# Sorting the columns of K and P by head inside VectorE's transposes (decode attention plus MLP, one core)

## The chip, the cores and the metric

The kernel runs on one core of a Trainium2 chip. The metric is the device time of one execution in microseconds (us); a kernel's time is the median of several executions. A core has TensorE (PE: matmuls, with PEld for the loading of their weights), VectorE (DVE), ScalarE (ACT), GpSimd (POOL) and SyncE (SP, which here issues most of the DMAs and waits for them). Each works through its own instructions in order and waits for the others at semaphores.

## The reference

One token (x has 1024 values) goes through an attention branch and an MLP branch, and both are added to x. The sizes are fixed: 32 query heads, 4 heads of K and V (8 query heads share one), 128 values per head, and the last 4096 positions of the cache.

```python
D, Hq, Hkv, Sk, Dh, F = 1024, 32, 4, 65536, 128, 3584
W = min(4096, max(256, Sk // 4))            # 4096
xn = layernorm(x)
q = (xn @ wq).reshape(1, 1, Hq, Dh).transpose(0, 2, 1, 3)
k = repeat(k_cache[:, :, Sk - W:, :], 8, axis=1)
v = repeat(v_cache[:, :, Sk - W:, :], 8, axis=1)
p = softmax(einsum("bhqd,bhkd->bhqk", q, k) * Dh ** -0.5)
a = einsum("bhqk,bhkd->bhqd", p, v).transpose(0, 2, 1, 3).reshape(1, 1, Hq * Dh) @ wo
y = layernorm(xn)
b = gelu(y @ w1 + b1) @ w2 + b2
out = x + a + b
```

## The kernel before, in words

Everything that is loaded is used once: w1, w2 (7 MB each), wq, wo (8 MB each), and 4 MB each of K and V, some 40 MB in all. The order of the loads is written out by hand on SP's queue. W1, K and wq are issued at the start; w2 (into w1's place) and V when the rows of w1 are done; wo (into wq's place, in pieces of 20, 8, 3 and 1 rows) when the rows of q are done.

**How K lies.** The window of 4096 keys is cut into 32 stretches (m) of 128 keys (b). Partition m*4+g holds stretch m of head g: 128 keys of 128 values. So every group of 32 partitions holds eight stretches of all four heads. VectorE's transpose works on blocks of 32 by 32; for TensorE the 128 values of a key (four pieces, e, of 32) must lie along the partitions. `turn_k` (L320, the transpose itself at L325) does it in eight instructions (n) of 16 keys each, 2048 columns: a block of 32 partitions (m, g) by 32 values becomes 32 partitions (values) by 32 columns (m, g). The columns of KD are then in the order n, e, b, m, g, so that the four heads alternate from column to column. KD and the loaded K (KR) share the space KV, shifted by one instruction's 2048 columns, so that each transpose writes over what the one before it has read.

**Scores.** `scores(g)` (L468) does for one head eight matmuls (L472, through the helper line L333) of 512 columns each, into bank g of PSUM. The view KG (L466) picks head g: every fourth column of KD. The stationary side is LB, a block pattern of q that lines L445 and L446 write. Ahead of that the rows of q are copied out of PSUM (L419 on ACT, L421 on DVE), turned on TensorE (L425), copied to QT (L429) and spread (L435).

**Softmax.** The maximum over the columns (L488), its transpose on TensorE (L478), the maximum over the pieces (L494, L499), its spread (L483) and the bias (L505) go in two halves of two heads each. Then ACT takes the exponentials, one instruction of 512 columns for each head (L510), and writes them as bf16 into Pb: column x*4+g for head g, so every fourth column. The sums go into SUMS on the way.

**P times V.** Two transposes on VectorE (L540, 1024 columns each) turn Pb's blocks of 32 by 32 into PT, and eight instructions (L546 on DVE, L547 on ACT) gather and mask them into PG, the stationary side of the product with V. The loop over V (`pv_rows`) follows. Its result goes through L579, L582 and L589, and L595 writes it as OT, two columns for each value of the heads, into VEC. L575 is a matmul into a bank that is not read. Last is the loop over wo (seven trips of four rows, and four rows behind it), which waits for the pieces of wo through SP (L600).

**The order around the change.** On VectorE: the GELU of the MLP (to L408), the eight K transposes, L421, L429, L445, the maxima, the P transposes, half of the gathering, L582, L595. On TensorE: the rows of w1, the rows of q, the q transposes, the scores with the maxima's small matmuls between them, the loop over w2, the loop over V, the loop over wo. On ACT: L419, L446, L499 and L505, the exponentials of the first half, L499 of the second half, L505, the exponentials of the second half, half of the gathering.

Of the kernel before, what the change touches and what calls it, by code (L numbers as in the profile page):

```python
# [7 lines left out]
ACTF = mybir.ActivationFunctionType  # L8
# [5 lines left out]
HKV = 4  # L14
# [14 lines left out]
NB = W // MB // 2  # L29
# [22 lines left out]
def bass_parallel_sum__sliding_block_cached__mixer_channel_mlp__decode_kernel(  # L52
# [18 lines left out]
    pe, dve, act, pool, sp = nc.tensor, nc.vector, nc.scalar, nc.gpsimd, nc.sync  # L71
# [12 lines left out]
    DVE = Track(nc, "S_DVE")  # L84
# [49 lines left out]
    KD = KV[:, 0:HKV * W]  # L134
    KR = KV[:, 2048:2048 + HKV * W]
    V = KV[:, 2048 + HKV * W:2048 + 2 * HKV * W]
    Pb = KV[:, HKV * W:HKV * W + 2048]
    PT = KV[:, 0:2048]
# [6 lines left out]
    PS = nc.alloc_psum_tensor("PS", [128, 8 * 512], f32)  # L145
# [11 lines left out]
    C = {}  # L157
# [94 lines left out]
    def fold(out, at, n):  # L252
# [9 lines left out]
        out=SAME[:, :].rearrange("p (h q) -> p h q", q=4), in0=HD[:, 112:120].unsqueeze(2).to_broadcast([128, REP, 4]),  # L262
# [52 lines left out]
    C["y"] = DVE.mark(dve.tensor_scalar(out=YTb[:, 0:KC], in0=YT16[:, 0:8], scalar1=msy[:, 2:3], scalar2=msy[:, 7:8],  # L315
                                        op0=ALU.subtract, op1=ALU.mult))
    C["zq"] = C["zo"] = DVE.mark(dve.memset(PS[:, 4 * 512:8 * 512], 0.0))
    KD4 = KD.rearrange("p (n e b s) -> p n b e s", n=8, e=4, b=16)

    def turn_k(n):  # L320
        if n == 0:
            dve.wait_ge(s_k, 16)
        else:
            dve.wait_ge(DVE.sem, DVE.cnt)
        C["kd"] = DVE.mark(dve.transpose(  # L325
            out=KD4[:, n], in_=KR[:, n * 2048:(n + 1) * 2048].rearrange("p (b e s) -> p b e s", b=16, e=4)))


    def lowered(ap, weights):
# [12 lines left out]
    def full(out, lhsT, rhs, load, start=False):  # L342
        return tile(out, lhsT, rhs, (128, 128), (0, 0), load, start)
# [42 lines left out]
    for i in range(8):  # L386
        n = 128 if i < 4 else 96
# [4 lines left out]
    for b, c in ((0, 4), (1, 3)):  # L392
# [16 lines left out]
        out=GT, in0=HT[:, :].unsqueeze(2).to_broadcast([128, FC, 2]), in1=U2[:, :].unsqueeze(2).to_broadcast([128, FC, 2]),  # L409
        op=ALU.mult))  # L410

    for n in range(8):
        turn_k(n)
# [49 lines left out]

    pe.wait_ge(DVE.sem, C["lb", 1])
    pe.wait_ge(ACT.sem, C["lb", 3])
    KG = KD.rearrange("p (n e x g) -> p e g n x", n=8, e=4, g=HKV)  # L466

    def scores(g):  # L468
        for c in range(2):
            for e in range(4):  # L470
                at = (e * HKV + g) * WIN + 8 - 8 * c
                last = full(PS[:, g * 512:(g + 1) * 512], LB[:, at:at + 128],  # L472
                            KG[:, e, g, 4 * c:4 * c + 4, :], True, c + e == 0)
        C["sc"] = PE.mark(last)
# [28 lines left out]
    def weigh(half):  # L503
        act.wait_ge(PE.sem, C["mxb"])
        C["bias"] = ACT.mark(act.activation(  # L505
            out=BIAS[:, 2 * half:2 * half + 2], in_=PS[:, 6 * 512 + 128 + 2 * half:6 * 512 + 130 + 2 * half],
            func=ACTF.Copy, scale=-SCALE))
        act.wait_ge(ACT.sem, C["bias"])
        for g in range(2 * half, 2 * half + 2):
            C["exp"] = ACT.mark(act.activation(  # L510
                out=Pb.rearrange("p (x g) -> p g x", g=HKV)[:, g, :], in_=PS[:, g * 512:(g + 1) * 512], func=ACTF.Exp,
                bias=BIAS[:, g:g + 1], scale=SCALE, accum_out=SUMS[:, g:g + 1]))

    scores(0)
# [6 lines left out]
    take_max(1)  # L521
    spread_max(0)
    weigh(0)
    sp.wait_ge(PE.sem, C["q"])
    load_rows(WA, wo_p, WO_CHUNKS, D, s_wo)
# [6 lines left out]
    join_max(1)  # L532
    spread_max(1)
    weigh(1)
    PT4 = PT.rearrange("p (b u c h) -> p b u c h", u=2, c=2, h=REP)[:, :, 0]
    PG4 = PG.rearrange("p (b c g h) -> p g b c h", c=2, g=HKV, h=REP)
    HB = NB // 2
    dve.wait_ge(ACT.sem, C["exp"])
    for half in range(2):
        C["tr", half] = DVE.mark(dve.transpose(out=PT[:, half * 1024:(half + 1) * 1024], in_=Pb[:, half * 1024:(half + 1) * 1024]))  # L540
    for half, eng, track in ((0, act, ACT), (1, dve, DVE)):
        eng.wait_ge(DVE.sem, C["tr", half])
        for g in range(HKV):
# [8 lines left out]
        out=SUMX[:, :].rearrange("p (g r) -> p g r", g=HKV), in0=SAME[:, :].unsqueeze(1).to_broadcast([128, HKV, 32]),  # L552
# [28 lines left out]
    for c in range(1, 2):  # L581
        C["d_od"] = DVE.mark(dve.scalar_tensor_tensor(  # L582
            out=OD[:, :], in0=PS[:, 4 * 512 + 128 * c:4 * 512 + 128 * c + 128], scalar=BLK[:, c:c + 1], in1=OD[:, :],
# [4 lines left out]
    for dq in range(4):  # L588
# [7 lines left out]
        out=OT, in0=PS[:, 6 * 512 + 160:6 * 512 + 192].unsqueeze(2).to_broadcast([128, 32, 2]), scalar1=REC[:, 0:1], scalar2=None, op0=ALU.mult))  # L596
# [55 lines left out]
```

## Time and profile before

| | |
|---|---|
| time, median of 3 runs | 103.63 us (103.58 to 103.99) |
| the profiled execution's own time | 102.51 us, span 101.1 us |
| busy, share of the span | PE 49.6 us (49%), DVE 32.4 (32%), PEld 20.5 (20%), ACT 15.1 (15%), POOL 9.1 (9%) |
| read from memory | 39.86 MB, 394 GB/s over the span |
| chain that ended last | DMA 84%, PE 10%, issue 2% |
| eight K transposes (L325) | 18.5 us busy, 2311 ns each |
| 32 score matmuls (L333, KV and LB) | 14.7 us busy, 57.67 to 72.40 us |
| four exponentials (L510) | 5.2 us busy, 1400 ns each |
| two P transposes (L540) | 2.4 us busy, 1224 ns each |

The span runs from the first to the last instruction, and the execution's own time has a little more on both sides. Times in the trace are microseconds from the start of the span. In a line of the profile, `out<-in` names the tensors, then come partitions by elements and type, and how often; the idle time of the engine ahead of it stands with what ended it. KV is the space that K, V and P share, WW the one for the weight matrices, PS is PSUM. The helper line L333 stands for every matmul that `tile`, `put` and `full` issue, so that these are told apart by their tensors.

### The profile page before, as it was taken

Reading aid. Unit: us, or ns where it says so; the run is one execution under the profiler, and the core shown is the slowest. Engines: PE = TensorE matmul, PEld = TensorE weight load, DVE = VectorE, ACT = ScalarE, POOL = GpSimd, SP = SyncE. Lnnn points to the kernel's source line nnn. Section 1 sums busy time; section 2 is a strip of 40 time slices with the busy share of each in tenths; the row PEclk is TensorE's granted clock in tenths of the full one; section 3 lists DMA queues with packets and bytes.
Section 4 is the critical chain, followed back from the end, with each engine's and each line's share of the span. In section 5 each row is a group of like instructions: output and inputs, shape, how many; then the busy total and the mean of one; then the engine's idle time right before and its main releaser. Section 6 shows DMA issues by size and latency. Waiting matters only on the chain.

```text
span 101.1 us, 1321 instructions
## 1 busy us (share of the span) xinstructions
PE 49.6 (49%) x523; PEld 20.5 (20%) x460; DVE 32.4 (32%) x42; ACT 15.1 (15%) x29; POOL 9.1 (9%) x33
## 2 busy tenths in 40 slices
PE   0000031579510000000496499999818857799672
PEld 0000031123110000000121222222215434445441
DVE  0000003360069999999202400221320760011000
ACT  0400000510400000000002200001298470010001
POOL 2000002599400000000000000000000100000000
PEclk9999999999998555555569976999995799999999
DMA  9888899599999999999999889999999699699400
GB/s 340 386 366 363 364 408 659 230 415 415 428 609 415 415 415 415 415 415 415 408 658 386 363 363 408 512 415 428 415 467 502 275 518 502 263 447 384 167 0 1
DMA packets 1340, 39.86 MB, mean 394 GB/s; under 512 B 182, under 2 KB 186, under 8 KB 444
## 3 DMA queue, kind: packets, MB, share of 16 engines
q1 hardware_dynamic: 1300, 39.85, 91.9%
q10 hardware_dynamic: 40, 0.01, 0.0%
HBM read 39.86 MB, written 0.00 MB: 394 GB/s over the span
## 4 chain that ended last, share of the span: by engine, by line
DMA 84%; PE 10%; issue 2%; SPq 1%; ACT 0%
DMA WW<-in_A_wq_dram 47%; DMA WW<-in_A_wo_dram 37%; PE PS L333 10%; SPq L203 1%; SPq L211 0%; ACT ORow L617 0%; SPq L196 0%; SPq L369 0%; SPq L600 0%
## 5 line engine op out<-in xcount | busy, mean ns | idle before, releaser
L325 DVE STREAM_TRANSPOSE KV<-KV 128x2048 bf16<-128x2048 bf16 x8 | 18.5, 2311 | 0.2
L333 PE MATMUL PS<-WW,XNTb 128*32 x64 | 5.2, 481 | 21.3 <-SPq L369 21.3
L333 PE MATMUL PS<-KV,LB 128*128 128x512 bf16 x32 | 14.7, 630 | 1.0 <-DVE LB L445 1.0
L333 PE MATMUL PS<-WW,VEC 128*32 (+1 forms) x240 | 10.2, 309 | 2.5 <-issue 2.3
L288 PE MATMUL PS<-oneb,XBR 1*128 1x1 bf16 x8 | 0.6, 196 | 13.8 <-DMA XBR<-in_A_x_dram 13.8
L333 PEld LDWEIGHTS PS<-WW,VEC 128*32 (+1 forms) x236 | 5.7, 105 | 7.2 <-issue 6.9
L333 PE MATMUL PS<-WW,YTb 128*32 x56 | 5.8, 542 | 1.6 <-DMA WW<-in_B_w_dram 1.6
L333 PE MATMUL PS<-KV 128*64 x64 | 5.0, 278 | 2.3 <-issue 1.2
L333 PEld LDWEIGHTS PS<-WW,XNTb 128*32 x32 | 1.1, 104 | 25.0 <-issue 25.0
L488 DVE TENSOR_REDUCE MXP<-PS 128x2 f32<-128x1024 f32 x2 | 2.4, 1224 | 10.8 <-PE PS L333 10.8
L333 PEld LDWEIGHTS PS<-KV,LB 128*128 128x128 bf16 x32 | 3.6, 116 | 10.8 <-issue 9.7
L510 ACT ACTIVATE KV<-PS,BIAS 128x512 bf16<-128x512 f32 x4 | 5.2, 1400 | 0.1
L551 POOL TENSOR_TENSOR SUMX<-SAME,SUMS 128x128 f32<-128x128 f32 x1 | 0.4, 401 | 52.3 <-ACT KV L510 52.3
L291 DVE COPY XT<-PS 128x8 f32<-128x8 f32 x1 | 0.2, 166 | 14.4 <-PE PS L288 14.4
L419 ACT ACTIVATE Hs<-PS 128x512 bf16<-128x512 f32 x1 | 0.6, 598 | 25.5 <-PE PS L333 25.5
L540 DVE STREAM_TRANSPOSE KV<-KV 128x1024 bf16<-128x1024 bf16 x2 | 2.4, 1224 | 4.6 <-ACT KV L510 4.6
L333 PEld LDWEIGHTS PS<-KV 128*64 x64 | 2.9, 109 | 4.2 <-issue 4.2
L288 PEld LDWEIGHTS PS<-oneb,XBR 1*128 1x128 bf16 x8 | 0.6, 160 | 13.7 <-issue 13.7
L582 DVE SCALAR_TENSOR_TENSOR OD<-PS,BLK,OD 128x128 f32<-128x128 f32 x1 | 0.4, 351 | 7.9 <-ACT OD L579 7.9
L333 PEld LDWEIGHTS PS<-WW,YTb 128*32 x32 | 1.6, 117 | 6.0 <-issue 5.7
L547 ACT ACTIVATE KV<-KV,GM 128x512 bf16<-128x512 bf16 x4 | 2.6, 710 | 1.3 <-DVE KV L540 1.3
L421 DVE CAST Hs<-PS 128x512 bf16<-128x512 f32 x1 | 0.7, 692 | 6.0 <-PE PS L333 6.0
(90 smaller groups left out, 40.0 us busy)
## 6 DMA issues: line engine op xcount, KB each, us to landing
WW<-in_B_w_dram SPq DMA_DIRECT2D x2, 7168.0 KB, 29.5
WW<-in_A_wo_dram SPq DMA_DIRECT2D x1, 5120.0 KB, 33.3
KV<-in_A_k_cache_dram SPq DMA_DIRECT2D x1, 4096.0 KB, 28.7
KV<-in_A_v_cache_dram SPq DMA_DIRECT2D x1, 4096.0 KB, 49.0
WW<-in_A_wo_dram SPq DMA_DIRECT2D x1, 2048.0 KB, 37.8
WW<-in_A_wo_dram SPq DMA_DIRECT2D x1, 768.0 KB, 39.2
WW<-in_A_wo_dram SPq DMA_DIRECT2D x1, 256.0 KB, 39.3
KV<-in_B_b_dram ACTq DMA_DIRECT2D x1, 7.0 KB, 8.8
```

Of the source, the lines that this page charges most:

```text
L203: sp.dma_start(dst[:, :], cache[0, :, SK - W:SK, :].rearrange("g (m b) d -> m g (b d)", m=MB),).then_inc(semaphore, 16)
L288: last = pe.matmul(xt[:, r:r + 1], lhsT=XBR[0:1, r:D:KC], rhs=oneb[0:1, 0:1])
L325: C["kd"] = DVE.mark(dve.transpose(out=KD4[:, n], in_=KR[:, n * 2048:(n + 1) * 2048].rearrange("p (b e s) -> p b e s", b=16, e=4)))
L333: return pe.add_instruction(mybir.InstMatmult(name=nc.get_next_instruction_name(), engine=pe.engine, ins=[lowered(rhs, False), lowered(lhs ...
L419: C["a_qs"] = ACT.mark(act.activation(out=Qs[:, 0:512], in_=PS[:, 6 * 512:7 * 512], func=ACTF.Copy))
L421: C["d_qs"] = DVE.mark(dve.tensor_copy(Qs[:, 512:1024], PS[:, 7 * 512:8 * 512]))
L488: C["mx", half] = DVE.mark(dve.tensor_reduce(out=MXP[:, 2 * half:2 * half + 2], in_=PS[:, half * 1024:(half + 1) * 1024].rearrange("p (g x ...
L510: C["exp"] = ACT.mark(act.activation(out=Pb.rearrange("p (x g) -> p g x", g=HKV)[:, g, :], in_=PS[:, g * 512:(g + 1) * 512], func=ACTF.Exp ...
L540: C["tr", half] = DVE.mark(dve.transpose(out=PT[:, half * 1024:(half + 1) * 1024], in_=Pb[:, half * 1024:(half + 1) * 1024]))
L547: else act.activation(out=dst, in_=src, func=ACTF.Copy, scale=GM[:, g:g + 1]))
L551: C["sumx"] = POOL.mark(pool.tensor_tensor(out=SUMX[:, :].rearrange("p (g r) -> p g r", g=HKV), in0=SAME[:, :].unsqueeze(1).to_broadcast([ ...
L582: C["d_od"] = DVE.mark(dve.scalar_tensor_tensor(out=OD[:, :], in0=PS[:, 4 * 512 + 128 * c:4 * 512 + 128 * c + 128], scalar=BLK[:, c:c + 1] ...
```

## The change

The columns of K and P are sorted by head. In KD the order is now n, e, g, b, m: the 128 columns of one head in one piece lie side by side. The K transpose reads as before and scatters what it writes: of the 32 columns of a block, eight runs over m of the four heads, each element goes 128 columns (256 bytes) from the one before it, and after four heads it goes on with the next m. The score matmuls read runs of 128 columns. The exponentials write 512 columns of Pb side by side for each head. The P transposes read across the four heads (512 columns, 1024 bytes, from one element to the next) and write PT in the order that it had. No instruction is added, removed or moved.

```diff
-    KD4 = KD.rearrange("p (n e b s) -> p n b e s", n=8, e=4, b=16)
+    KD4 = KD.rearrange("p (n e g b m) -> p n b e m g", n=8, e=4, g=HKV, b=16)
...
         C["kd"] = DVE.mark(dve.transpose(
-            out=KD4[:, n], in_=KR[:, n * 2048:(n + 1) * 2048].rearrange("p (b e s) -> p b e s", b=16, e=4)))
+            out=KD4[:, n], in_=KR[:, n * 2048:(n + 1) * 2048].rearrange("p (b e m g) -> p b e m g", b=16, e=4, g=HKV)))
...
-    KG = KD.rearrange("p (n e x g) -> p e g n x", n=8, e=4, g=HKV)
+    KG = KD.rearrange("p (n e g x) -> p e g n x", n=8, e=4, g=HKV)
...
             C["exp"] = ACT.mark(act.activation(
-                out=Pb.rearrange("p (x g) -> p g x", g=HKV)[:, g, :], in_=PS[:, g * 512:(g + 1) * 512], func=ACTF.Exp,
+                out=Pb[:, g * 512:(g + 1) * 512], in_=PS[:, g * 512:(g + 1) * 512], func=ACTF.Exp,
                 bias=BIAS[:, g:g + 1], scale=SCALE, accum_out=SUMS[:, g:g + 1]))
...
     for half in range(2):
-        C["tr", half] = DVE.mark(dve.transpose(out=PT[:, half * 1024:(half + 1) * 1024], in_=Pb[:, half * 1024:(half + 1) * 1024]))
+        C["tr", half] = DVE.mark(dve.transpose(
+            out=PT[:, half * 1024:(half + 1) * 1024].rearrange("p (b m g) -> p b m g", b=HB, g=HKV),
+            in_=Pb.rearrange("p (g b m) -> p b m g", g=HKV, b=NB)[:, half * HB:half * HB + HB]))
```

## The prediction, made before the changed kernel had run

> **What bounds the kernel now.** I read the chain of waits first, then the DMA issues, the timeline around the first wait that the change can reach, the groups by shape, and the granted clock by window. The chain that ended last, in order of time:
>
> ```profile
> 1.91 47.34 DMA WW<-in_A_wq_dram
> ...
> 49.54 5.19 PE PS L333 x62
> ...
> 55.13 37.78 DMA WW<-in_A_wo_dram
> ...
> 93.03 0.62 PE PS L333 x16
> ```
>
> The chip loads memory almost without a break: wq, then 5.2 us of q rows on TensorE, then wo. But the last DMA link is only one of two that end together. Wo comes in four pieces (the DMA issues: size, us from issue to landing; the first and last piece shown, the second takes 37.8):
>
> ```profile
> WW<-in_A_wo_dram SPq DMA_DIRECT2D x1, 5120.0 KB, 33.3
> ...
> WW<-in_A_wo_dram SPq DMA_DIRECT2D x1, 256.0 KB, 39.3
> ```
>
> Issued from 54.75 us on, the first piece (20 of 32 rows, five trips of the wo loop) lands at 88.1, the second at 92.9, the last (issued 56.1) at 95.4. The loop began at 93.03, because attention's last step (OT, L595) ended only at 92.35 and the matmul queued behind it on TensorE (L575, which nothing waits for) at 92.85; the timeline:
>
> ```profile
> 91.95 0.40 DVE L595 TENSOR_SCALAR VEC<-PS,REC 128x64 bf16<-128x64 f32 x1 [1.10 <-PE PS L589]
> ...
> 93.03 0.62 PE L333 MATMUL PS<-WW,VEC 128*32 x16 [0.17 <-SPq L600]
> ```
>
> So a longer attention path lengthens the kernel one for one, while a shorter one soon meets the loads: the last row needs the piece of 95.4, so TensorE could end at about 95.8 instead of 99.33. **The most that can be gained is 3.5 us.** Attention needs the transposed K from VectorE, which has room only here (the timeline of VectorE alone):
>
> ```profile
> 30.03 18.73 DVE L325 STREAM_TRANSPOSE KV<-KV 128x2048 bf16<-128x2048 bf16 x8
> 54.76 0.69 DVE L421 CAST Hs<-PS 128x512 bf16<-128x512 f32 x1 [6.00 <-PE PS L333]
> ```
>
> The eight K transposes are busy until 48.76. Next in VectorE's order is the copy of half of q (L421), which waits for TensorE until 54.76: 6.00 us of slack. Behind it are queued the q transposes, the QT copy, LB and, from 57.67, the score matmuls.
>
> **The change part by part.** No instruction is added or removed; four kinds of access change.
>
> *Score matmuls (L472).* 32 run from 57.67 to 72.40, one every 0.452 us. The windows give a granted clock of 0.50 at 59.5 to 61.5 and 1.00 from 63 on; the pitch is the same in both, so the stride of four elements sets it. Adjacent 512-column reads are the q rows, eight in two rounds of four column groups: a loop step took 0.43 us at full clock (52.43 to 52.86) and 0.80 at half (51.63 to 52.43), 0.215 and 0.40 a round. The q rows began at half clock and were at full after 2.8 us. If the scores do the same: 7 at 0.40 and 25 at 0.215 = 8.2 us against 14.73. Saved 6.5 (bounds: all at half clock 1.9, all at full 7.8). All of it is on the path.
>
> *Exponentials (L510).* The groups by shape (busy us in all, mean ns of one, idle before), for this and the two parts behind it:
>
> ```profile
> L325 DVE STREAM_TRANSPOSE KV<-KV 128x2048 bf16<-128x2048 bf16 x8 | 18.5, 2311 | 0.2
> ...
> L510 ACT ACTIVATE KV<-PS,BIAS 128x512 bf16<-128x512 f32 x4 | 5.2, 1400 | 0.1
> ...
> L547 ACT ACTIVATE KV<-KV,GM 128x512 bf16<-128x512 bf16 x4 | 2.6, 710 | 1.3 <-DVE KV L540 1.3
> ...
> L595 DVE TENSOR_SCALAR VEC<-PS,REC 128x64 bf16<-128x64 f32 x1 | 0.4, 395 | 1.1 <-PE PS L589 1.1
> ...
> L429 DVE COPY QT<-PS 128x32 bf16<-128x32 bf16 x1 | 0.2, 227 | 0.7 <-PE PS L425 0.7
> ```
>
> L510 writes every fourth bf16 and takes 1400 ns; L547, as wide and also with a per-partition operand, writes runs of eight and takes 710. So an exponential drops by 0.69 us. The first two: the copy L499 for the second half sat behind them until 75.31, though its maximum was ready at 74.31, so 0.95 us comes off. The last two (1.38 us) shorten the path to the gathered P, but TensorE's w2 loop runs beside it and ends at 82.58, against 82.78 for gathered P: only 0.2 us is to be had there.
>
> *P transposes (L540).* After the change they read one bf16 from each of four places 1024 bytes apart. No row shows VectorE reading so. Bounds: as before, or the dearest scattered write below (2.8 ns an element). The second gather ended at 82.49. With 1.38 us off and both transposes unchanged, w2 decides: 0.2 us gained. At 2.8 ns (1.78 us more each) it ends at 84.67: 1.9 us lost. I take the middle price, 2.18 ns (1.15 us more each): 82.49 - 1.38 + 2.30 = 83.41, 0.6 us lost.
>
> *K transposes (L325): the term that decides.* From 1224 ns for 1024 elements (L540) and 2311 for 2048 (L325): 1.06 ns an element and 0.137 us fixed, plus 0.03 between two. Before, each block writes 32 adjacent bf16 (64 bytes). After the change each bf16 is followed by one 256 bytes further (the next head), and after four it goes back. No row shows a transpose that writes so. The rows that write lone bf16:
> - ACT, L510, steps of 8 bytes: 0.836 ns (its slope, from 384 ns for 256 columns and 598 for 512) + (1400-710)/512 = 2.18 ns an element.
> - DVE, L429 (four hops of 8 bytes, then back by one element): its fixed part from L291, an 8-element copy of 166 ns, 166-8x1.06 = 157.5; (227-157.5)/32 = 2.17.
> - DVE, L595 (hops of 62 bytes and 4): fixed part from L582, 351 ns for 128 adjacent elements with one per-partition operand too, 351-128x1.06 = 215; (395-215)/64 = 2.81. L408, which writes the same way, gives 2.82 (316 ns, 56 elements, fixed 158 from L399, 188 for 28).
>
> Bounds are 1.06 (hops are free; below that nothing goes, since the same elements are moved) and 2.8. I take 2.18: L429's visiting order is the nearest, four hops and back by one element, and ACT's row agrees. A transpose then takes 0.137 + 2048x2.18 ns = 4.60, with the gap 4.63 instead of 2.34. Eight: 18.3 us more, 6.0 of it in the slack: **12.3 us on the path** (at 2.8 ns: 5.90 each, 22.5 us; at 1.06: none). This wait moves to L421, with everything queued behind it.
>
> The Trainium skill (Vector Engine (DVE) Microarchitecture Reference, "Measured stream behaviour on trn2") speaks against this change: a port keeps full rate only for runs of two or more adjacent 4-byte words; it measured 1.71 ns an element for 4-byte outputs hopping 4 KiB every element, and 2.50 for a step of 24 words. L429 and L595 agree that lone writes cost more; no row shows hops as far as 4 KiB. By 1.71 my estimate is 3.67 us a transpose, 4.6 on the path, and the sum would end 2.2 us faster; by 2.50, 17.6 on the path and 10.7 us slower.
>
> **Sum.** +12.3 (K) - 6.5 (scores) - 0.95 (first exponentials) + 0.6 (P) = +5.5 us. From gathered P on, 15.7 us to the end stay as they are, since wo has landed by then. The profiled execution took 102.51 (span 101.1), 1.1 below the median of 103.63; added to the median: **109.1 us**. The savings are 6.85 us together, so no change in time needs 12.85 us on eight transposes: 3.95 us each, 1.85 ns an element.
>
> **The rivals.**
> - *Scattered writes are cheap in a transpose* (below 1.85 ns): the 6.00 us of slack takes most or all of it, attention gets ahead, and the loads become the bound: 3.5 us gained, 100.1 us; the full gain holds up to 1.63 ns, and between 1.63 and 1.85 part of it is gained. For it: the hops are long and regular and each 16 bytes are returned to soon. Against: both engines' rows of lone bf16 writes lie above 2.1 ns. The skill's 1.71 (the page above) falls here. Chance 0.26, and 0.04 for a landing within 0.5% of now.
> - *The reads of K don't get faster*: 0.452 us stays, set by something else in the weight and matmul pairs. Then 12.3 - 0.95 + 0.6 = +12.0: 115.6 us. Against: the pitch didn't move when the clock doubled, while adjacent q rows halved. Chance 0.10.
> - *The forecast*, K's writes decide: 0.60. Its own range is 1.9 ns (7.7 on the path, +0.9 us: 104.5) to 2.8 ns with P's reads as dear (22.5 - 6.5 - 0.95 + 1.9 = +17: 120.6).
>
> **How the numbers follow.** Faster 0.26, same 0.04, slower 0.10 + 0.60 = 0.70; 0.5% (0.5 us) is about what a measurement of this kernel can tell from no change. The faster case is more than 2 in 10, so the range must hold it: from 99.9 (the loads' limit and the spread of the runs) to 119, leaving out the dearest writes.
>
> **What would show it.** Each K transpose near 4.6 us, the last ending near 67 instead of 48.76; L421 starting right behind it, with no wait for TensorE; score matmuls 0.2 to 0.4 us apart; exponentials near 0.71; the wo loop starting near 98.5 with no wait for a load. Wrong if L325 stays under 3.9 us: then the wo loop would wait for its pieces at 88.1 and 92.9. Wrong in size if L325 comes out above 5 us, or if the score matmuls keep 0.45.

## The result: 146.4 us, and the profile after

The changed kernel takes 146.41 us (median of 6 runs, 146.02 to 146.94) against 103.38 before (6 runs, 102.59 to 103.99): 1.417 times, 95% interval 1.410 to 1.424. The profiled execution took 146.02 us, its span 144.6 against 101.1.

The groups by shape, the same ones that the prediction read (busy us in all, mean ns of one, idle before it):

```profile
L325 DVE STREAM_TRANSPOSE KV<-KV 128x2048 bf16<-128x2048 bf16 x8 | 74.4, 9294 | 0.2
...
L333 PE MATMUL PS<-KV,LB 128*128 128x512 bf16 x32 | 8.6, 433 | 1.0 <-DVE LB L445 1.0
...
L540 DVE STREAM_TRANSPOSE KV<-KV 128x1024 bf16<-128x1024 bf16 x2 | 3.8, 1948 | 2.5 <-ACT KV L510 2.5
...
L510 ACT ACTIVATE KV<-PS,BIAS 128x512 bf16<-128x512 f32 x4 | 2.7, 682 | 0.1
```

A K transpose went from 2311 to 9294 ns. The score matmuls and the exponentials moved about as forecast; a P transpose went from 1224 to 1948 ns, less than the 2.37 us forecast. The chain that ended last now runs through VectorE, here at its first and last K transpose and behind:

```profile
30.53 9.11 DVE KV L325
...
95.67 9.28 DVE KV L325
...
108.13 6.79 PE PS L333 x24
...
115.03 1.73 PE PS L333 x8
```

Before, wq and wo held most of this chain and L325 wasn't in it. The timeline shows what queues behind the last transpose:

```profile
30.35 74.60 DVE L325 STREAM_TRANSPOSE KV<-KV 128x2048 bf16<-128x2048 bf16 x8
...
104.58 0.88 DVE L421 CAST Hs<-PS 128x512 bf16<-128x512 f32 x1
105.52 0.77 PEld L425 LDWEIGHTS PS<-identb,Hs 128*128 128x128 bf16 x8 [51.32 <-DVE Hs L421]
```

ACT's half of the same copy (L419) ran at 54.93, so q was ready then. VectorE's half had no idle time before it and came at 104.58: 49.65 us on the path, with TensorE idle throughout. All loads had landed by 95.5, before the scores began.

### The profile page after: what moved, and what is told of

Same layout as the page of the kernel before. It is cut to its first block, busy times and chain, and to the rows that moved or that the text cites. A ratio compares the mean times of both kernels' runs of the same rounds, so it can differ in the third digit from the quotient of the medians.

```text
span 144.6 us, 1321 instructions
## 1 busy us (share of the span) xinstructions
PE 45.1 (31%) x523; PEld 21.9 (15%) x460; DVE 89.5 (62%) x42; ACT 12.9 (9%) x29; POOL 9.1 (6%) x33
## 4 chain that ended last, share of the span: by engine, by line
DVE 57%; PE 21%; DMA 13%; ACT 4%; issue 3%
DVE KV L325 51%; PE PS L333 17%; DMA WW<-in_B_w_dram 13%; DVE KV L540 3%; ACT KV L510 2%; PE PS L577 1%; DVE KV L548 1%; PE PS L425 1%; PE PS L591 1%; DVE LB L445 1%; PE PS L483 0%; PE PS L388 0%; ACT Hs L372 0%; DVE Hs L421 0%; ACT Hs L373 0%
## 5 line engine op out<-in xcount | busy, mean ns | idle before, releaser
L325 DVE STREAM_TRANSPOSE KV<-KV 128x2048 bf16<-128x2048 bf16 x8 | 74.4, 9294 | 0.2
L425 PE MATMUL PS<-identb,Hs 128*128 128x128 bf16 x8 | 1.0, 311 | 50.6 <-DVE Hs L421 50.6
L333 PE MATMUL PS<-KV,LB 128*128 128x512 bf16 x32 | 8.6, 433 | 1.0 <-DVE LB L445 1.0
L425 PEld LDWEIGHTS PS<-identb,Hs 128*128 128x128 bf16 x8 | 0.8, 141 | 51.3 <-DVE Hs L421 51.3
L488 DVE TENSOR_REDUCE MXP<-PS 128x2 f32<-128x1024 f32 x2 | 2.4, 1224 | 6.6 <-PE PS L333 6.6
L333 PE MATMUL PS<-KV 128*64 x64 | 5.8, 349 | 1.8 <-issue 1.8
L446 ACT ACTIVATE LB<-PS 32x256 bf16<-32x256 f32 x2 | 0.8, 376 | 51.7 <-PE PS L435 51.7
L540 DVE STREAM_TRANSPOSE KV<-KV 128x1024 bf16<-128x1024 bf16 x2 | 3.8, 1948 | 2.5 <-ACT KV L510 2.5
L333 PEld LDWEIGHTS PS<-KV 128*64 x64 | 4.2, 137 | 3.2 <-issue 2.6
L419 ACT ACTIVATE Hs<-PS 128x512 bf16<-128x512 f32 x1 | 0.6, 597 | 25.3 <-PE PS L333 25.3
(90 smaller groups left out, 43.5 us busy)
```

The lines of the kernel that those rows point to most:

```text
L325: C["kd"] = DVE.mark(dve.transpose(out=KD4[:, n], in_=KR[:, n * 2048:(n + 1) * 2048].rearrange("p (b e m g) -> p b e m g", b=16, e=4, g=HKV)))
L333: return pe.add_instruction(mybir.InstMatmult(name=nc.get_next_instruction_name(), engine=pe.engine, ins=[lowered(rhs, False), lowered(lhs ...
L425: last = pe.matmul(PSb[:, 7 * 1024 + 128 * i: 7 * 1024 + 128 * (i + 1)], lhsT=Qs[:, i * 128:(i + 1) * 128], rhs=identb[:, :], is_transpose ...
L446: else act.activation(out=dst, in_=src, func=ACTF.Copy))
L488: C["mx", half] = DVE.mark(dve.tensor_reduce(out=MXP[:, 2 * half:2 * half + 2], in_=PS[:, half * 1024:(half + 1) * 1024].rearrange("p (g x ...
```

## The experiments

The theory after the result was that a lone bf16 written to SBUF costs far more than the rows of the trace before had suggested. Its rivals were that the transpose itself can't stand a scattered output, that the hop of 256 bytes meets one bank again and again, and that the early return to the same place is dear.

**One part at a time (e2, e3).** The first keeps the old K4, KG and K transpose and has the new exponentials and P transposes; the second is the reverse.

```diff
 e2_p_alone, against the changed kernel
-    KD4 = KD.rearrange("p (n e g b m) -> p n b e m g", n=8, e=4, g=HKV, b=16)
+    KD4 = KD.rearrange("p (n e b s) -> p n b e s", n=8, e=4, b=16)
...
-    KG = KD.rearrange("p (n e g x) -> p e g n x", n=8, e=4, g=HKV)
+    KG = KD.rearrange("p (n e x g) -> p e g n x", n=8, e=4, g=HKV)
 e3_k_alone, against the kernel before: the same lines the other way round
```

> Only P's columns are sorted (exponentials side by side, P transposes reading across the heads); K, its transposes and the scores are as before. Theory that K's scattered writes carry the whole loss and P's part is a small gain: the first two exponentials take 0.95 us off the path, the P transposes (1.95 instead of 1.22 us each) give 0.1 to 0.2 back: 102.6 us where the kernel before has 103.4. Rival, P's strided reads cost more than the exponentials save: 103.4 to 104.1.

> Only K's columns are sorted (scattered transposes, scores reading runs of 128); P as before. Theory that K's scattered writes carry the loss: 147.2 us (the changed kernel's 146.4 with the exponentials' 0.95 back and the P transposes' 0.15 off), each K transpose at 9.28 us. Rival, both scattered sides share the loss: well under 146.

P alone: 102.39 us against 103.06 in the same set, ratio 0.992 (0.988 to 0.997), a small gain of the size expected. K alone: 147.58 us, ratio 1.425 (1.412 to 1.437), each transpose at 9279 ns. So K's side carries the whole loss and P's is worth 0.7 us. In P alone the groups show both sides of that trade:

```profile
L540 DVE STREAM_TRANSPOSE KV<-KV 128x1024 bf16<-128x1024 bf16 x2 | 3.8, 1950 | 2.7 <-ACT KV L510 2.7
...
L510 ACT ACTIVATE KV<-PS,BIAS 128x512 bf16<-128x512 f32 x4 | 2.7, 682 | 0.1
```

**The disputed cost by itself (e1).** Trials placed behind VectorE's last step; each writes 1024 columns from adjacent ones. In the code, `hop(x)` writes four places x columns apart and then goes on by one column, and `hop(128, run)` writes runs of adjacent columns with the change's hop between them.

```diff
+    def trial(op, out, in_):
+        dve.wait_ge(DVE.sem, DVE.cnt)
+        DVE.mark((dve.transpose if op else dve.tensor_copy)(out=out, in_=in_))
...
+    trial(1, S[:, 0:1024], IN)
+    for x in (8, 16, 32, 64, 128, 132, 256, 512, 2048):
+        trial(1, *hop(x))
+    for step in (2, 4, 8, 24):
+        trial(1, S[:, 0:1024 * step:step], IN)
+    for run in (2, 4, 8):
+        trial(1, *hop(128, run))
...
+    for step in (1, 2, 4, 8):
+        for i in range(12):
+            full(PS[:, 0:512], LB[:, 0:128], V[:, 0:512 * step:step], True, True)
```

> The kernel before with trials behind it that its result does not use: VectorE transposes and copies of 1024 bf16 columns from adjacent columns into a spare space, with different steps of the output (hop x: four places x columns apart, then on by one column, as the heads lie in the change, x = 128; step s: every s-th column, no return; run r: r adjacent columns, then the hop of 128), transposes of 1024 4-byte elements, two ACT copies, and 12 matmuls each that read every 1st, 2nd, 4th and 8th column. Theory A (the write port's price for a lone bf16, whatever the instruction): the copy at hop 128 takes about as long as the transpose there, both near 4.46 ns an element (4.7 us), and runs of 8 are free (1.2 us). Theory B (the transpose's own: it does not stand a scattered output): the copy at hop 128 stays at 2.2 to 2.8 ns an element (2.4 to 3.0 us), while the transpose is near 4.7 us at every hop and step. Theory C (hops of a power of two fall into one bank): hop 132 is at 2.8 ns or less (3 us), hop 128 at 4.46. Theory D (a 16-byte piece that is returned to four writes later is the dear case): steps without return of 8 and 24 are near 2.5 ns, hops with return near 4.46. Matmuls: every 4th column near 0.45 us, every column near 0.22, every 2nd in between or at 0.22.

Single instructions of the timeline of VectorE (start, us): the transpose at the change's hop of 256 bytes, at a step of 8 and of 16 bytes, in runs of two bf16 with a hop of 256 bytes, the copy at the hop of 256 bytes, and the transpose of 4-byte elements at a hop of 512 bytes.

```profile
113.73 4.78 DVE L602 STREAM_TRANSPOSE WW<-WW 128x1024 bf16<-128x1024 bf16 x1
...
138.98 2.44 DVE L602 STREAM_TRANSPOSE WW<-WW 128x1024 bf16<-128x1024 bf16 x1
...
141.46 4.70 DVE L602 STREAM_TRANSPOSE WW<-WW 128x1024 bf16<-128x1024 bf16 x1
...
151.10 1.25 DVE L602 STREAM_TRANSPOSE WW<-WW 128x1024 bf16<-128x1024 bf16 x1
...
157.83 2.73 DVE L602 COPY WW<-WW 128x1024 bf16<-128x1024 bf16 x1
...
172.97 1.93 DVE L602 STREAM_TRANSPOSE WW<-WW 128x1024 f32<-128x1024 f32 x1
```

All trials, us for 1024 columns (matmuls: us from one start to the next, 512 columns):

| what is written or read | us |
|---|---|
| transpose, bf16, adjacent | 1.25 |
| hop of 16, 32, 64, 128 bytes | 4.77, 4.55, 4.72, 4.85 |
| hop of 256, 264 bytes | 4.78, 4.78 |
| hop of 512, 1024, 4096 bytes | 4.72, 4.73, 4.73 |
| step of 4, 8, 16, 48 bytes, no return | 1.32, 2.44, 4.70, 4.87 |
| runs of 2, 4, 8, then a hop of 256 bytes | 1.25, 1.25, 1.25 |
| transpose, 4-byte elements: adjacent, hop of 256, 512 bytes | 1.25, 1.92, 1.93 |
| VectorE copy: adjacent; hop of 16, 256, 264, 4096 bytes | 0.43; 2.40, 2.73, 2.45, 2.73 |
| VectorE copy, step of 8, 48 bytes | 1.30, 2.51 |
| ACT copy: adjacent, hop of 256 bytes | 1.06, 4.81 |
| matmul that reads every 1st, 2nd, 4th, 8th column | 0.216, 0.226, 0.452, 0.900 |

From 99 us on no load ran beside these trials (DMA share 0.00 in the windows), so the loads aren't what makes the scattered writes slow. Bank and early return fall at once: 264 bytes cost a transpose what 256 do, and steps of 16 and 48 bytes without return cost as much as hops with it. What counts is how many writes fall into the same 16 bytes in a row: at 4 bytes four of them (1.32 us), at 8 bytes two (2.44), from 16 bytes on one (4.7). Taking off the fixed 0.137 us, that is 4.5 ns for each 16-byte piece visited. It needs lone bf16: runs of two bf16 cost nothing extra, and lone 4-byte elements cost 1.74 ns. Reads by TensorE fit the same picture with another price: 0.90 us for 512 pieces is 1.76 ns a piece, two columns in each halve it, four quarter it. VectorE's copy at the hop of 256 bytes came out as theory B had it (2.73 us, where A said 4.7); ACT's copy there, and the transposes at steps of 4 and 8 bytes and in runs, speak against B. Left open was why VectorE's copy is half as dear as a transpose.

**The same, sharpened (e7).** The diff replaces the list of trials by transposes in runs of two in every 16 bytes, from an even and an odd column, transposes that read with steps, copies from PSUM, and ACT copies of 256 columns.

```diff
+    F32 = PS[:, 0:1024]
...
+    trial(1, *runs(2, 0))
+    trial(1, *runs(2, 1))
+    trial(1, *runs(4, 1))
...
+    trial(1, S[:, 0:1024], WW[:, 2048:2048 + 8192:8])
...
+    for step in (2, 4, 8, 16, 24):
+        trial(0, S[:, 0:1024 * step:step], F32)
...
+    for step in (1, 2, 4, 8):
+        act.wait_ge(ACT.sem, ACT.cnt)
+        ACT.mark(act.activation(out=S2[:, 0:256 * step:step], in_=WW[:, 0:256], func=ACTF.Copy))
```

> The kernel before with more trials behind it that its result does not use. VectorE transposes of 1024 bf16 columns: written in runs of 2 in every 16 bytes, from an even column and from an odd one, and in runs of 4 from an odd one; read at every 4th, 8th and 16th column; copies from PSUM (fp32) to bf16 at every 1st, 2nd, 4th, 8th, 16th and 24th column and in runs of 2 from an even column; ACT copies of 256 columns at every 1st, 2nd, 4th and 8th column. Theory P (price by 16-byte piece: 1.75 ns read or whole words, 4.5 ns with lone bf16; the copies in the first set were half as dear because they ran through two ports): runs of 2 from an even column 1.25 us; from an odd one, two half words, 2.3 us or more; reads at every 4th 1.25 us, at every 8th and 16th 1.9; copies from PSUM, which can't use two ports, 1.1 to 1.3, 1.3, 2.4, 4.7, 4.7, 4.7, and 1.2 in runs of 2; ACT 0.38, 0.46, 0.75, 1.3. Rival (a copy's write is cheaper than a transpose's by its nature): copies from PSUM stay at 2.4 to 2.7 from the 8th column on.

Two of the copies from PSUM, at steps of 8 and 16 bytes:

```profile
106.63 2.42 DVE L603 CAST WW<-PS 128x1024 bf16<-128x1024 f32 x1
...
109.09 4.68 DVE L603 CAST WW<-PS 128x1024 bf16<-128x1024 f32 x1
```

The full row is 1.23, 1.29, 2.42, 4.68, 4.43 and 4.85 us for the six steps, and 1.23 in runs of two: the price of the transposes, so nothing in the transpose is special. Copies within SBUF are the exception, with 2.4 to 2.7 us against 4.4 to 4.9, and with 0.43 us against 1.23 for adjacent columns; why they are cheaper isn't shown here. Runs of two took 1.25 us from an even column and 2.41 from an odd one, where the same two bf16 are halves of two different words: 512 pieces at 4.4 ns. Runs of four from an odd column took 1.29. Reads took 1.25 us at every 4th column and 2.00 and 2.02 at every 8th and 16th, 1.82 ns a piece, a little over the 1.9 us expected. ACT took 0.42, 0.50, 0.78 and 1.37 us.

**Two writes to a piece, inside the kernel (e6).**

```diff
-    KD4 = KD.rearrange("p (n e g b m) -> p n b e m g", n=8, e=4, g=HKV, b=16)
+    KD4 = KD.rearrange("p (n e x g k) -> p n e x k g", n=8, e=4, g=HKV, k=4)
...
+        for e in range(4):
...
+            C["kd"] = DVE.mark(dve.transpose(out=KD4[:, n, e].rearrange("p (b j) k g -> p b j k g", j=2), ...
...
```

> As the changed kernel, but the heads alternate in runs of four columns in KD, so that an element lies 8 bytes from the one before and two successive writes share a 16-byte piece; a K transpose is cut into four of 512 columns each (32 in all), because the pattern has one dimension too many otherwise. Theory P: 4.5 / 2 = 2.25 ns an element, 0.137 + 512 x 2.25 = 1.29 us each; 32 x 1.32 = 42.2 us, 17.5 us on the path against 6.6 saved: 114 us. The scores read four columns of each piece: 0.216 to 0.226 us apart. Rival (a price for each scattered element, wherever it goes): 4.46 ns, 2.42 us each, 78 us, 150 us.

```profile
L328 DVE STREAM_TRANSPOSE KV<-KV 128x512 bf16<-128x512 bf16 x32 | 41.0, 1282 | 1.3 <-DMA KV<-in_A_k_cache_dram 0.2
```

114.59 us, ratio 1.106 (1.100 to 1.113), with 1282 ns against the 1290 expected: (1282 - 137)/512 = 2.24 ns, half of the change's 4.46. The price by piece holds inside the kernel too, with K turned in place.

**Whole runs of eight (e4).** K is loaded so that eight stretches of one head lie on adjacent partitions; one load then becomes four of 32 partitions each.

```diff
-    load_cache(KR, A_k_cache, s_k)
+    for q in range(4):
+        sp.dma_start(
+            KR[32 * q:32 * q + 32, :],
+            A_k_cache[0, :, SK - W + 1024 * q:SK - W + 1024 * q + 1024, :].rearrange("g (m b) d -> g m (b d)", m=8),
+        ).then_inc(s_k, 16)
...
-    KD4 = KD.rearrange("p (n e g b m) -> p n b e m g", n=8, e=4, g=HKV, b=16)
+    KD4 = KD.rearrange("p (n e g b m) -> p n b e g m", n=8, e=4, g=HKV, b=16)
...
```

> As the changed kernel, but K is loaded in four pieces so that eight stretches of one head lie on adjacent partitions: the transpose then writes runs of eight bf16 (16 bytes), hopping 256 bytes between runs, and the scores read runs of 128 as in the change. If lone bf16 are the dear thing (A, C, D): K transposes 2.3 us each, done at about 49, scores near 0.22 us, and the loads become the bound: 100.1 us, or up to 1.5 later if four loads of 32 partitions take longer than one. If a transpose does not stand any scattered output (B): 9 us each, 146 us.

The time came out far off what was expected, and the transposes as expected. The timeline of VectorE:

```profile
99.88 18.73 DVE L329 STREAM_TRANSPOSE KV<-KV 128x2048 bf16<-128x2048 bf16 x8 [68.38 <-DMA KV<-in_A_k_cache_dram]
```

Eight transposes in 18.73 us, the time of the kernel before, with 256-byte hops between runs of 16 bytes. But K landed at about 99.9 us instead of 30.0, and wq 114.8 us after its issue instead of 47.3: 168.86 us, ratio 1.635 (1.623 to 1.646). The bandwidth in the page's slices from 29 to 100 us is 76 to 267 GB/s, where the kernel before mostly has 360 to 430. The semaphore events of this trace say more: each of the four loads of K ends with four completions, near 40, 60, 80 and 100 us, where the one load of K had sixteen. Of wq's sixteen, twelve come by 60.5 us and four at 118.5 to 118.9. This fits K's loads going one after another through the same four of the sixteen DMA engines, which then held up their share of wq. A packet of 64 KB also took about 5.0 us between 20 and 60 us, instead of 2.4 in the changed kernel; why stays open.

**Whole words (e5), the version that beats both.** Two adjacent bf16 are transposed as one 4-byte element. Each VectorE instruction has half the elements, none of its writes is half a word, and the values of a pair lie in adjacent columns of KD, so that the scores read every second column.

```diff
-    KD4 = KD.rearrange("p (n e g b m) -> p n b e m g", n=8, e=4, g=HKV, b=16)
+    KD4 = KD.bitcast(f32).rearrange("p (n e g b m) -> p n b e m g", n=8, e=2, g=HKV, b=16)
+    KR4 = KR.bitcast(f32)
...
-            out=KD4[:, n], in_=KR[:, n * 2048:(n + 1) * 2048].rearrange("p (b e m g) -> p b e m g", b=16, e=4, g=HKV)))
+            out=KD4[:, n], in_=KR4[:, n * 1024:(n + 1) * 1024].rearrange("p (b e m g) -> p b e m g", b=16, e=2, g=HKV)))
...
-    KG = KD.rearrange("p (n e g x) -> p e g n x", n=8, e=4, g=HKV)
+    KG = KD.rearrange("p (n e g x t) -> p e t g n x", n=8, e=2, g=HKV, t=2)
...
+    for e in range(2):                                     # the spread of q in the same order
+        POOL.mark(pool.tensor_copy(
+            REP4[:, 256 * e:256 * e + 256].rearrange("p (t q d) -> p t q d", t=2, q=4),
+            identf[:, 64 * e:64 * e + 64].rearrange("p (d t) -> p t d", t=2).unsqueeze(2).to_broadcast([128, 2, 4, 32])))
```

> As the changed kernel, but the K transposes take two adjacent bf16 as one 4-byte element: 1024 elements an instruction, each written lone, 512 bytes from the one before. The scores read every second column, and the spread of q (REP4) is ordered to match. Theory P (a 16-byte piece of a partition that is visited costs 1.75 ns if it is read or if whole 4-byte words are written, and 4.5 ns if lone bf16 are written): 0.137 + 1024 x 1.74 = 1.92 us a transpose, less than the 2.31 before; scores 0.226 us apart; attention ends 6 to 8 us earlier, and the kernel ends with the loads: 3.0 to 3.5 us off, 99.6 to 100.1 us. Rival (scattered output is dear in these transposes whatever the size of the element): 4.46 ns an element, 4.7 us a transpose, 13 us on the path against 6.6 saved: 110 us.

99.11 us (99.00 to 99.34) against 103.73 in the same set: ratio 0.956 (0.952 to 0.960), a little less time than the 99.6 to 100.1 us expected. The timeline:

```profile
30.21 15.57 DVE L327 STREAM_TRANSPOSE KV<-KV 128x1024 f32<-128x1024 f32 x8
...
54.93 0.69 DVE L423 CAST Hs<-PS 128x512 bf16<-128x512 f32 x1 [9.15 <-PE PS L335]
...
57.84 5.59 PE L335 MATMUL PS<-KV,LB 128*128 128x512 bf16 x24 [0.96 <-DVE LB L447]
...
77.04 5.38 PE L335 MATMUL PS<-KV 128*64 x56 [2.47 <-DMA KV<-in_A_v_cache_dram]
...
85.29 0.39 DVE L599 TENSOR_SCALAR VEC<-PS,REC 128x64 bf16<-128x64 f32 x1 [1.10 <-PE PS L593]
...
88.69 0.62 PE L335 MATMUL PS<-WW,VEC 128*32 x16 [2.49 <-SPq L604]
```

A transpose takes 1.92 us, and VectorE's slack ahead of q's copy grows from 6.00 to 9.15 us. OT is ready at 85.68 instead of 92.35, after a wait for V that is new too. Then the wo loop waits for its first piece, and the chain ends with the last one:

```profile
56.28 39.36 DMA WW<-in_A_wo_dram
...
95.68 0.30 PE PS L335 x4
```

By the timeline TensorE ends at 95.95, against 99.33 before, and the last piece of wo lands at 95.64: the loads are the bound. Attention got 6.7 us shorter and 3.4 of it counts.

## Why the prediction was wrong, by its own steps

**Right: where it would be decided.** The K transposes left their slack, L421 started behind them without a wait for TensorE, everything behind it moved, and no load was waited for at the end.

**Right in size: the small terms but one.** Scores from first to last took 8.63 us (108.13 to 116.76; 8.2 was forecast): saved 6.1 against 6.5. An exponential takes 0.68 us (0.71), and from the end of the scores to the w2 loop it is 2.99 us instead of 3.96: 0.97 saved (0.95). From w2's start to the loop over V it is 7.45 instead of 7.31: 0.14 lost, where 0.6 was forecast with 2.18 ns an element; a P transpose takes 1.95 us, 1.77 ns. That price had been borrowed from writes, while here only the reads are scattered. From there to TensorE's end it is 15.66 us before and 15.64 after, where no change was forecast. The measured sum: 49.65 (K) + 0.17 (q ended later) + 0.64 (the steps from L421 to the scores) - 6.1 - 0.97 + 0.14 = 43.5, the difference of the spans.

**Wrong: the price of a K transpose, the step "I take 2.18".** It forecast 4.60 us each and 12.3 on the path; measured are 9.28 and 49.65. The upper bound of 2.8 ns was as wrong: 4.46. The times were read correctly; the fault was to take their price as one for each element. It is one for each 16-byte piece, and every row that I used put several elements into a piece in a row:
- L510 writes every 8 bytes, two to a piece: 2 x 2.18 = 4.36 ns a piece.
- L429 writes four places 8 bytes apart within 32 bytes, two to a piece if QT starts on a 16-byte boundary: 2 x 2.17 = 4.34.
- L595 and L408 write at 0 and 62 bytes in each 66. If VEC starts on a 16-byte boundary, the write at 62 and the next one at 66 share a piece in six of eight cases, so 16 elements make 10 visits: 2.81 x 16/10 = 4.50.

The change visits another piece with every element. The number of e1 and e7, 4.5 ns, thus stood in these rows of the trace before, behind a count that wasn't made. L510 and L429 agreed with each other because both put two to a piece, and that agreement was taken for a general price; only L595 and L408, which put fewer to a piece, pointed to a dearer one. With 4.5 ns the sum would have been 0.137 + 2048 x 4.5 = 9.35 us each, 50.3 us on the path, and 103.63 + 50.3 - 6.85 = 147.1 us.

**The rivals.** "The reads of K don't get faster" fell: in the changed kernel successive score matmuls start 0.43 us apart at a granted clock of 0.50 and 0.216 apart at 1.00, and in e1 the pitch follows the step. "Scattered writes are cheap" fell for bf16, yet its end was right: with whole words (e5) the transposes fit into the slack and the loads stop the gain, with a profiled execution of 99.00 us, 3.5 below the one before, as that case had it.

**The rule that was weighed.** The Trainium skill (Vector Engine (DVE) Microarchitecture Reference, "Measured stream behaviour on trn2") has 1.71 ns for lone 4-byte writes that hop far; e1's 4-byte transposes agree, at 1.74. It has no row for 2-byte elements, and there the price is 2.6 times that. Its 2.50 for a step of 24 words isn't borne out or refuted here, since no 4-byte trial had that step. The Trainium skill (SBUF — State Buffer, Specifications (TRN2)) speaks of 16-byte lines that want at least two hits each for full bandwidth. VectorE's reads agree (two to a piece are free, one costs 1.8 ns). TensorE's reads don't (two columns to a piece took 0.452 us, twice the 0.216 of adjacent ones), and the bf16 writes don't (two cost 2.25 ns an element).

## What to carry to other kernels

Price a strided access by how many 16-byte pieces of a partition it visits and by whether it writes whole 4-byte words, not by its elements, and count for each row of the trace how many elements it puts into a piece before carrying its price over. Where the scattering can't be avoided, let it fall on the reading side or on whole 4-byte words: two adjacent bf16 moved as one element turned a loss of 43 us into a gain of 4.6. And look first at where the gain would stop: here the loads allowed 3.5 us in the profile, whatever attention saved.

## What was not expected of the hardware

- A lone bf16 written to SBUF costs 4.2 to 4.6 ns for each 16-byte piece it falls into, on VectorE (transposes, and copies from PSUM) and on ACT alike; a whole 4-byte word costs 1.74 ns, and two bf16 that fill an aligned word come without extra cost. Starting the same runs of two on an odd column took 2.41 us instead of 1.25. Why half a word is so dear can't be seen here.
- The length of the hop hardly matters: from 16 bytes to 4 KiB a transpose of 1024 columns took 4.55 to 4.85 us.
- TensorE's reads have a price by piece as well: 0.216 us for 512 adjacent columns at full clock, 0.226 at every second, 0.452 at every fourth, 0.900 at every eighth. In e1 the last pitch stayed the same when the granted clock went from 1.00 (104.4 to 108.0 us) to 0.50 (109.5 to 114.3 us).
- A 4-byte transpose moves twice the bytes of a bf16 one in the same time: 1.25 us for 1024 adjacent elements in both.
